# Query weights written in overlapping groups of four columns, and 22 agents copied with shifts from rows four partitions apart

## The chip, the cores and the metric

The kernel runs on one core of one Trainium2 chip. A core has five engines with a queue of instructions each: TensorE (PE in the profile; its weight loads, PEld, run beside its matmuls), VectorE (DVE), ScalarE (ACT), GpSimd (POOL) and SyncE (SP, which here issues all but one of the DMA transfers), and 16 DMA engines that carry the transfers. The metric is the time of one execution in microseconds. Three runs of the kernel before gave 426.61, 426.80 and 429.79 us; their median is 426.8 us.

## The reference

Agent attention, then a gated convolution, for 4 batches of 12800 rows of 128 channels, 49 agents and 5 taps. What is computed, in float32:

```
def sm(a, b):
    s = scale * (a @ b.transpose(0, 2, 1))
    s = s - s.max(-1, keepdims=True)
    e = np.exp(s)
    return e / (e.sum(-1, keepdims=True) + 1e-09)
a2k = sm(agents, k)
agent_v = a2k @ v
q2a = sm(q, agents)
x = q2a @ agent_v
...
for k in range(K):
    gate_pre += conv_w[k][None, None, :] * xp[:, k:k + S, :]
gate = 1.0 / (1.0 + np.exp(-gate_pre))
val = x @ w_val
return gate * val @ w_out
```

`xp` is `x` with four rows of zeros ahead of it: tap k reads a row k - 4 back.

## The kernel before, in words

**Units and chunks.** A batch is cut into 10 units of 1280 rows for the attention and 25 chunks of 512 rows for the convolution. Two units make a segment of 2560 rows, which is five chunks.

**The two halves.** For each batch, keys and values are first reduced to 49 agent vectors (`key_scores`, `key_max`, `agent_values`). `fold_weights` then multiplies these vectors with the taps and with the value weights, so that gate and value come from the query weights (49 numbers a row) directly, without x itself. The keys and values of batch b + 1 run among the chunks of batch b.

**Two-part numbers.** The folded weights and the query weights w are each written as a float16 high part and a float16 rest, and three of the four products are summed: high with high, low with high, high with rest. With 128 rows of one tile, x1, a matmul covers the low part of w (49 rows), its high part (49 rows), and a second copy of the high part for as many agents as still fit (30 rows). The other 19 agents' high parts, for the product with the weights' rest, lie in a second tile, x2, each five times, shifted by 0 to 4 columns: 95 rows, so that one matmul does all five taps. A gate chunk is thus five matmuls with x1 (line 922) and one with x2 (line 926); a value chunk is one with each (949, 953). The output projection is three more (992 to 994), on hh and hl, the two parts of h.

**One unit of queries** (`queries`): scores on TensorE, a transpose and a maximum on VectorE, subtraction on GpSimd, exp on ScalarE, sums and division on VectorE into qw. Then pt, the tile of 128 columns, is filled: the high part by ScalarE (line 779), the second copy by GpSimd (784), the low part by GpSimd as w less the high part (794).

**Transposes and shifts.** The first four units' pt is transposed on TensorE, the others' by a DMA transpose from pt into x1 (line 835). When both units of a segment have landed, two DMAs on SP's queue copy the 19 agents with their shifts from x1 into x2 (`shifts`, line 884): 15 rows three partitions apart, then 4 neighbouring rows, each row read five times. This is called the shift pair here; the profile shows it as x<-x. (For the first four units there is a pair for every unit, of half the width.) A halo copy of four columns goes on GpSimd from one segment's x1 to the next one's (819); it waits for the transpose of the segment's second unit.

**What sets the order.** TensorE's order is written out by hand in a string. The instructions of all other engines and of SP's queue are put in order by a planner (`Plan.order`), which simulates the engines with a cost in microseconds that each step names; other costs give another order. Each queue then runs strictly in its order. SP's queue holds the loads of keys, queries and values (ld, a ring of 11), the transposes, the shift pairs and the writes of the output (ob).

Of the kernel before, what the change touches and what calls it, by code (L numbers as in the profile page):

```python
# [9 lines left out]
F32 = mybir.dt.float32  # L10
# [3 lines left out]
ALU = mybir.AluOpType  # L14
# [3 lines left out]
P = 128  # L18
G = 4
BLK = 32  # L20
AP_ = 64

UNIT = 1280
NBLK = 10
# [8 lines left out]
THREES = 15  # L33
NDUP = 2 * THREES
X2R = 19
X2CUTS = ((0, THREES, 3, 0.5), (THREES, X2R, 1, 0.3))
# [140 lines left out]
def tile_agent_attention_gated_conv(  # L177
# [39 lines left out]
    qw = ring(NPT, [P, NBLK, A], F32, "qw")  # L217
# [43 lines left out]
    tiny = const.tile([P, NBLK], F32, name="tiny")  # L261
    nc.scalar.dma_start(out=ag_sb, in_=agT)
# [5 lines left out]
    nc.vector.memset(tiny, 1e-9 / QS)  # L268
    nc.vector.memset(x1s[0][:, 0:PAD], 0.0)
    for t in wst_sb:  # L270
        nc.gpsimd.memset(t[:, TAPS + 1 :, :], 0.0)
# [232 lines left out]
    avT = const.tile([P, A], F32, name="avT")  # L504
    mx = const.tile([P, 2], F32, name="mx")
    gw = const.tile([P, TAPS, A], F32, name="gw")
    gs = const.tile([P, TAPS, A], F32, name="gs")
# [5 lines left out]
    def fold_weights(b):  # L513
# [19 lines left out]
        def normalise():  # L533
            dve.tensor_scalar_add(den, pt[:, 0:A], 1e-9)
            dve.reciprocal(out=den, in_=den)
            dve.tensor_tensor(out=avT, in0=pt[:, AP_ : AP_ + A], in1=den, op=ALU.mult)
# [5 lines left out]
                out=gw, in0=avT.unsqueeze(1).to_broadcast([P, TAPS, A]),  # L542
                in1=conv_sb.unsqueeze(2).to_broadcast([P, TAPS, A]), op=ALU.mult,
# [4 lines left out]
        def gate_scale():  # L548
# [16 lines left out]
                out=pv[:, 0:A], lhsT=wval_sb, rhs=avT, start=True, stop=True  # L565
# [4 lines left out]
        x2g = wst[:, TAPS + 1, 0 : TAPS * X2R].rearrange("p (r k) -> p k r", k=TAPS)  # L570
        x2v = wst[:, TAPS + 2, 0 : TAPS * X2R].rearrange("p (r k) -> p k r", k=TAPS)
        ghi = wst[:, 0:TAPS, 0:A]
        vhi = wst[:, TAPS, 0:A]

        def threes(x):

            if len(x.shape) == 2:
                return x[:, 0 : 3 * THREES].rearrange("p (i r) -> p i r", r=3)
            return x[:, :, 0 : 3 * THREES].rearrange("p k (i r) -> p k i r", r=3)

        def rest(out, full, s, hi):
            dve.scalar_tensor_tensor(
                out=out, in0=full, scalar=rs[:, s : s + 1], in1=hi,
                op0=ALU.mult, op1=ALU.subtract,
            )

        def val_weights():
# [9 lines left out]
            dve.tensor_scalar_mul(vhi, pv[:, 0:A], rs[:, 1:2])  # L597
            pv3, hi3 = threes(pv[:, 0:A]), threes(vhi)
            rest(
                wst[:, TAPS, 2 * A :].rearrange("p (i r) -> p i r", r=2),  # L600
                pv3[:, :, 0:2], 1, hi3[:, :, 0:2],
            )
            rest(x2v[:, HALO, 0:THREES], pv3[:, :, 2], 1, hi3[:, :, 2])
            rest(x2v[:, HALO, THREES:], pv[:, 3 * THREES : A], 1, vhi[:, 3 * THREES :])

        def gate_weights():
            dve.tensor_scalar_mul(ghi, gw, rs[:, 0:1])
# [6 lines left out]
        def gate_rest_pool():  # L614
            def less(out, full, hi):
                nc.gpsimd.tensor_tensor(out=out, in0=full, in1=hi, op=ALU.subtract)

            gs3, hi3 = threes(gs), threes(ghi)
            twos = wst[:, 0:TAPS, 2 * A :].rearrange("p k (i r) -> p k i r", r=2)
            for r in range(2):  # L620
                less(twos[:, :, :, r], gs3[:, :, :, r], hi3[:, :, :, r])
            less(x2g[:, :, 0:THREES], gs3[:, :, :, 2], hi3[:, :, :, 2])
            less(x2g[:, :, THREES:], gs[:, :, 3 * THREES :], ghi[:, :, 3 * THREES :])

        def gate_rest():
            gw3, hi3 = threes(gw), threes(ghi)
            twos = wst[:, 0:TAPS, 2 * A :].rearrange("p k (i r) -> p k i r", r=2)
            for r in range(2):
                rest(twos[:, :, :, r], gw3[:, :, :, r], 0, hi3[:, :, :, r])
            rest(x2g[:, :, 0:THREES], gw3[:, :, :, 2], 0, hi3[:, :, :, 2])  # L630
            rest(x2g[:, :, THREES:], gw[:, :, 3 * THREES :], 0, ghi[:, :, 3 * THREES :])
# [3 lines left out]
        if b == 0:  # L635
            add("pool", 0.4, gate_scaled, ["gw", "rsg"], ["gs"])
            add("act", 0.4, lambda: nc.scalar.copy(out=ghi, in_=gs), ["gs"], [(*w_, "g")])
            add("pool", 1.0, gate_rest_pool, ["gs", (*w_, "g")], [(*w_, "r")])
        else:
# [4 lines left out]
            lambda: nc.scalar.copy(out=wst[:, 0:TAPS, A : 2 * A], in_=ghi),  # L644
# [3 lines left out]
            "act", 0.22, lambda: nc.scalar.copy(out=wst[:, TAPS, A : 2 * A], in_=vhi),  # L648
# [84 lines left out]
    def queries(b, u):  # L733
# [4 lines left out]
        sT, d, e, w, r, sm = sts[x], qw[g % NPT], qw[g % NPT], qw[g % NPT], qr[x], qsm[x]  # L738
# [23 lines left out]
        def sums():  # L762
# [14 lines left out]
        p_ = ("pt", g % NPT)  # L777
        add(
            "act", 0.58, lambda: nc.scalar.copy(out=pt[:, :, A : 2 * A], in_=w),  # L779
# [3 lines left out]
            "pool", 0.44,  # L783
            lambda: nc.gpsimd.tensor_scalar(
                out=pt[:, :, 2 * A :].rearrange("p n (i r) -> p n i r", r=2),
                in0=w[:, :, 0 : 3 * THREES].rearrange("p n (i r) -> p n i r", r=3)[:, :, :, 0:2],
                scalar1=1.0, scalar2=0.0,
                op0=ALU.mult, op1=ALU.add,
# [3 lines left out]
        add(  # L792
            "pool", 1.09,
# [393 lines left out]
```

## Time and profile before

| | |
|---|---|
| median of 3 runs | 426.8 us (426.61 to 429.79) |
| span of the profiled execution | 423.6 us |
| what the fastest run has beyond that span | 3.0 us |
| TensorE busy | 403.9 us, 95% |
| ScalarE busy | 301.5 us, 71% |
| VectorE busy | 293.3 us, 69% |
| GpSimd busy | 228.2 us, 54% |
| DMA | 127.62 MB, 301 GB/s on average |
| shift pair of a segment | 375 KB and 100 KB |

For the profiled execution there is no other time than its span, from its first to its last instruction; the runs' times have the start and the end around it too. Busy shares are means over stages: up to about 60 us the kernel waits for the first loads and the first fold, from then on TensorE has work nearly without a break. A matmul's end is modelled, and 512 columns are listed at about 380 ns though the next one starts about 216 ns later, so a busy TensorE is read from its holes, not from the sum of its durations. An idle time in brackets stands before the instruction, with what ended it.

### The profile page before, as it was taken

To read this page: it belongs to the slowest core of one execution; us is meant where nothing else is said; L and a number is where in the kernel's file an instruction comes from. 1 tells how busy PE (TensorE), PEld (TensorE's weight loads), DVE (VectorE), ACT (ScalarE), POOL (GpSimd) and SP (SyncE) were. 2 spreads that over 40 slices of the span, in tenths; PEclk is the share of its full clock that TensorE was granted. 3 is DMA by queue.
4 is the path that set the end of the run, shared out by engine and by line. 5 is a ranking of instruction groups with operands and counts; after the bars stand their busy time and mean duration, and the time that the engine had idled before them with its cause. 6 is when DMAs were issued, how large, how long until landed. Compare 5 with 4: busy or idle time off the path is not lost.

```text
span 423.6 us, 10042 instructions
## 1 busy us (share of the span) xinstructions
PE 403.9 (95%) x3907; PEld 197.0 (47%) x3907; DVE 293.3 (69%) x562; ACT 301.5 (71%) x521; POOL 228.2 (54%) x263
## 2 busy tenths in 40 slices
PE   4979999999999999999999899999999989999995
PEld 1358434346555443446555343335555534344443
DVE  3757899867875978667795575767765678676231
ACT  1564568779966777678876486778876567788776
POOL 1002557654657565554566355574366277877553
PEclk9969999999999999999999899999999999999998
DMA  8999999999999999999999999999999977755733
GB/s 320 420 417 411 370 367 353 301 295 310 412 293 283 346 317 362 304 278 356 351 379 324 271 299 370 314 332 302 296 393 322 239 196 161 199 163 176 205 121 124
DMA packets 75129, 127.62 MB, mean 301 GB/s; under 512 B 50466, under 2 KB 50850, under 8 KB 75084
## 3 DMA queue, kind: packets, MB, share of 16 engines
q1 hardware_dynamic: 74940, 126.87, 96.9%
q8 instruction: 30, 0.49, 0.5%
q10 hardware_dynamic: 144, 0.13, 0.2%
q14 instruction: 15, 0.12, 0.1%
HBM read 79.25 MB, written 26.21 MB: 249 GB/s over the span
## 4 chain that ended last, share of the span: by engine, by line
PE 78%; DMA 9%; DVE 8%; ACT 1%; POOL 1%; issue 1%; SPq 0%; POOLq 0%; DVEq 0%; ACTq 0%
PE gate L922 23%; PE sc L376 17%; PE av L480 10%; PE val L949 5%; PE out L992 5%; PE val L953 5%; PE gate L926 5%; PE out L993 4%; DMA ld<-kT 4%; PE out L994 4%; DMA x<-pt 3%; DMA x<-x 2%; DVE h L962 1%; DVE qw L772 1%; DVE qsm L763 1%
## 5 line engine op out<-in xcount | busy, mean ns | idle before, releaser
L973 POOL TENSOR_TENSOR hl<-h,hh 128x512 f16<-128x512 f32 (+1 forms) x101 | 116.9, 1158 | 96.1 <-ACT hh L968 96.0
L922 PE MATMUL gate<-x,stat 128*128 128x512 f16 (+1 forms) x500 | 125.2, 380 | 0.2 <-ACT th L935 0.2
L962 DVE SCALAR_TENSOR_TENSOR h<-th,val 128x512 f32<-128x512 f32 x100 | 67.8, 678 | 66.8 <-PE out L993 26.2
L376 PE MATMUL sc<-ld,ag_sb 128*32 128x320 f32 x1280 | 101.5, 447 | 7.6 <-DMA ld<-kT 7.0
L935 ACT ACTIVATE th<-gate,unscale 128x512 f32<-128x512 f32 x100 | 68.3, 683 | 33.3 <-PE gate L926 31.7
L1006 ACT ACTIVATE ob<-out,oscale 128x512 f32<-128x512 f32 x98 | 67.3, 687 | 21.3 <-PE out L994 20.1
L922 PEld LDWEIGHTS <-stat 128*128 128x128 f16 x505 | 46.3, 97 | 63.7 <-issue 14.8
L968 ACT CAST hh<-h 128x512 f16<-128x512 f32 (+1 forms) x101 | 61.5, 609 | 17.2 <-DVE h L962 16.4
L750 POOL TENSOR_TENSOR qw<-sT,qmx 128x490 f32<-128x490 f32 x40 | 41.4, 1035 | 47.6 <-DVE qmx L745 47.5
L376 PEld LDWEIGHTS sc<-ld,ag_sb 128*32 128x32 f32 x1280 | 36.7, 111 | 59.4 <-issue 25.7
L480 PE MATMUL av<-ld,eT 128*32 128x129 f32 (+1 forms) x1400 | 50.7, 279 | 1.0 <-DVE eT L386 1.0
L480 PEld LDWEIGHTS av<-ld,eT 128*32 128x32 f32 (+1 forms) x1400 | 47.1, 117 | 7.5 <-issue 2.5
L794 POOL TENSOR_TENSOR pt<-qw,pt 128x490 f16<-128x490 f32 x40 | 44.8, 1120 | 3.1 <-ACT pt L779 2.9
L471 ACT ACTIVATE e<-ks,kbias 128x320 f32<-128x320 f32 x80 | 39.3, 554 | 5.4 <-DVE eT L386 3.3
L386 DVE STREAM_TRANSPOSE sT<-sc 128x640 f32<-128x640 f32 x40 | 33.6, 839 | 13.4 <-PE sc L376 12.7
L402 ACT COPY ks<-sc 128x640 f32<-128x640 f32 x40 | 27.7, 691 | 21.2 <-PE sc L376 19.1
L386 DVE STREAM_TRANSPOSE eT<-e 128x640 f32<-128x640 f32 x40 | 33.5, 842 | 9.8 <-ACT e L471 5.2
L926 PE MATMUL gate<-x,stat 95*128 95x512 f16 x100 | 38.3, 383 | 1.5 <-DMA x<-x 1.5
L949 PE MATMUL val<-x,stat 128*128 128x512 f16 x100 | 38.2, 382 | 0.8 <-DVE h L962 0.6
L953 PE MATMUL val<-x,stat 95*128 95x512 f16 x100 | 38.1, 381 | 0.0
L994 PE MATMUL out<-hl,wo 128*128 128x512 f16 x98 | 37.0, 378 | 1.1 <-POOL hl L973 1.1
L992 PE MATMUL out<-hh,wo 128*128 128x512 f16 x98 | 37.3, 381 | 0.1
(130 smaller groups left out, 389.4 us busy)
## 6 DMA issues: line engine op xcount, KB each, us to landing
ld<-kT SPq DMA_DIRECT2D x40, 640.0 KB
ld<-qT SPq DMA_DIRECT2D x40, 640.0 KB
ld<-vP SPq DMA_DIRECT2D x39, 645.0 KB
outT<-ob SPq DMA_DIRECT2D x48, 512.0 KB
x<-x SPq DMA_DIRECT2D x18, 375.0 KB
x<-x SPq DMA_DIRECT2D x18, 100.0 KB
outT<-ob SPq DMA_DIRECT2D x3, 256.0 KB
x<-x SPq DMA_DIRECT2D x4, 187.5 KB
```

The source lines that it names most:

```text
L376: nc.tensor.matmul(out=out[g * BLK : (g + 1) * BLK, j, 0:GT], lhsT=ag_sb[:, b, j * BLK : (j + 1) * BLK], rhs=src[:, g * GT : (g + 1) * GT] ...
L386: nc.vector.transpose(out=out.rearrange("p n (j i) -> p j n i", j=2), in_=in_.rearrange("p j (n i) -> p j n i", i=BLK),)
L480: nc.tensor.matmul(out=av[o + j : o + j + cols, 0 : C + 1], lhsT=et[:, n, j : j + cols], rhs=vt[:, n, :], start=(u == 0 and n < 2), stop=( ...
L922: nc.tensor.matmul(out=pg, lhsT=stat[:, k, :], rhs=x1[:, c : c + w], start=(k == 0), stop=False,)
L926: nc.tensor.matmul(out=pg, lhsT=stat[0 : TAPS * X2R, TAPS + 1, :], rhs=x2[0 : TAPS * X2R, o2 : o2 + w], start=False, stop=True,)
L935: lambda: nc.scalar.activation(out=th, in_=pg, func=AF.Tanh, scale=unscale[:, 0:1]),
L949: nc.tensor.matmul(out=pv, lhsT=stat[:, TAPS, :], rhs=x1s[(b * NCH + n0 // CH) // 5 % NX][:, PAD + o2 : PAD + o2 + w], start=True, stop=False,
L953: nc.tensor.matmul(out=pv, lhsT=stat[0 : TAPS * X2R, TAPS + 2, :], rhs=x2[0 : TAPS * X2R, o2 : o2 + w], start=False, stop=True,)
L962: lambda: nc.vector.scalar_tensor_tensor(out=h, in0=th, scalar=1.0, in1=pv, op0=ALU.add, op1=ALU.mult),
L968: "act", 0.16 + 0.42 * scale, lambda: nc.scalar.copy(out=hh, in_=h),
L973: lambda: nc.gpsimd.tensor_tensor(out=hl, in0=h, in1=hh, op=ALU.subtract),
L1006: lambda: nc.scalar.activation(out=ob[:, o : o + w], in_=po, func=AF.Copy, scale=oscale),
```

## The change

**Columns of pt.** pt's 128 columns get another layout. The high part stands in 17 groups of four neighbouring columns, from column 32 on; group i holds w of agents 3i - 1, 3i, 3i + 1, 3i + 2. Neighbouring groups overlap by one agent, so 16 agents stand twice. ScalarE writes all 680 elements a partition in one instruction; qw gets a zero column ahead of w and two behind it for the ends of the groups (52 columns for 49). GpSimd writes 11 more second copies (agents 0, 3, ... 30) to columns 21 to 31, where 30 stood before. The low part goes to the 51 columns that are left, in two GpSimd instructions of 210 and 300 elements; the second overwrites two columns that the first reads.

**Shifts.** 27 agents now stand twice in x1, so 22 go to x2, 110 rows, from row 16 on: 16 rows four partitions apart, then 6 rows four partitions apart. x2's other rows are zeroed once, and its matmuls use all 128 rows.

**Weights.** The folded weights take the same places: 51 columns for 49, two ScalarE copies for each low part instead of one, four subtractions for the value's rest instead of three.

**Costs.** The planner gets 0.75 for 0.58 (ScalarE's copy), 0.3 for 0.44 and 1.3 for 1.09 (GpSimd), 0.5 and 0.2 a unit for 0.5 and 0.3 (the pair). The string of TensorE's order is the same.

```
-THREES = 15
-NDUP = 2 * THREES
-X2R = 19
-X2CUTS = ((0, THREES, 3, 0.5), (THREES, X2R, 1, 0.3))
+AW = 52
+HI = 32
+FOURS = 17
+LOWS = ((HI + 4 * FOURS - 2, 0, 10), (0, 10, FOURS - 10))
+TWICE = 11
+AGAIN = HI - TWICE
+X2R = 22
+X2O = 16
+X2CUTS = ((0, 16, HI + 2, 0.5), (16, X2R, HI + 1 + 4 * TWICE, 0.2))
+def fours(x):
+    return x[:, :, HI : HI + 4 * FOURS].rearrange("p n (i r) -> p n i r", r=4)
+def threes(x, first, n, width):
+    ap = [tuple(d) for d in x.ap]
+    return bass.AP(x.tensor, x.offset + first, ap[:2] + [(3, n), (1, width)])
...
     for t in wst_sb:
-        nc.gpsimd.memset(t[:, TAPS + 1 :, :], 0.0)
+        nc.gpsimd.memset(t, 0.0)
+    for t in x2s + qw:
+        nc.gpsimd.memset(t, 0.0)
...
+        def rests(full, hi, out, x2_, less):
+            n = X2R - 16
+            less(out[:, :, HI + 4 : HI + 4 * FOURS : 4], full[:, :, 2:A:3], hi[:, :, 0:16, 3])
+            less(out[:, :, AGAIN:HI], full[:, :, 0 : 3 * TWICE : 3], hi[:, :, 0:TWICE, 1])
+            less(x2_[:, :, 0:16], full[:, :, 1:A:3], hi[:, :, 0:16, 2])
+            less(x2_[:, :, 16:], full[:, :, 3 * TWICE : A : 3], hi[:, :, TWICE : TWICE + n, 1])
+        def lows(out, hi):
+            for to, i0, n in LOWS[::-1]:
+                nc.scalar.copy(
+                    out=out[:, :, to : to + 3 * n].rearrange("p k (i r) -> p k i r", r=3),
+                    in_=hi[:, :, i0 : i0 + n, 1:4],
+                )
...
-            "act", 0.58, lambda: nc.scalar.copy(out=pt[:, :, A : 2 * A], in_=w),
+        hi = fours(pt)
+            "act", 0.75, lambda: nc.scalar.copy(out=hi, in_=threes(wide, 0, FOURS, 4)),
...
-            "pool", 0.44,
+            "pool", 0.3,
             lambda: nc.gpsimd.tensor_scalar(
-                out=pt[:, :, 2 * A :].rearrange("p n (i r) -> p n i r", r=2),
-                in0=w[:, :, 0 : 3 * THREES].rearrange("p n (i r) -> p n i r", r=3)[:, :, :, 0:2],
-                scalar1=1.0, scalar2=0.0,
-                op0=ALU.mult, op1=ALU.add,
+                out=pt[:, :, AGAIN:HI], in0=w[:, :, 0 : 3 * TWICE : 3],
+                scalar1=1.0, scalar2=0.0, op0=ALU.mult, op1=ALU.add,
             ),
...
-            "pool", 1.09,
-            lambda: nc.gpsimd.tensor_tensor(
-                out=pt[:, :, 0:A], in0=w, in1=pt[:, :, A : 2 * A], op=ALU.subtract
-            ),
+        def lower():
+            for to, i0, n in LOWS[::-1]:
+                nc.gpsimd.tensor_tensor(
+                    out=pt[:, :, to : to + 3 * n].rearrange("p n (i r) -> p n i r", r=3),
+                    in0=threes(wide, 1 + 3 * i0, n, 3), in1=hi[:, :, i0 : i0 + n, 1:4], op=ALU.subtract,
+                )
+        add("pool", 1.3, lower, [("qw", g % NPT), (*p_, 0)], [(*p_, 1)])
...
-        for r0, r1, every, us in X2CUTS:
-            first = A + (2 if every == 3 else 3 * THREES)
-            rows = x1[first : first + 1 + (r1 - r0 - 1) * every : every, c : c + 1]
+        for r0, r1, first, us in X2CUTS:
+            rows = x1[first : first + 1 + (r1 - r0 - 1) * 4 : 4, c : c + 1]
...
-                    out=x2[r0 * TAPS : r1 * TAPS, o : o + n * UNIT],
+                    out=x2[X2O + r0 * TAPS : X2O + r1 * TAPS, o : o + n * UNIT],
...
-                out=pg, lhsT=stat[0 : TAPS * X2R, TAPS + 1, :],
-                rhs=x2[0 : TAPS * X2R, o2 : o2 + w], start=False, stop=True,
+                out=pg, lhsT=stat[:, TAPS + 1, :], rhs=x2[:, o2 : o2 + w],
+                start=False, stop=True,
```

**Where the order moves.** Three places. The first is SP's queue ahead of the shift pair of chunk 20 of the second batch; ld from qT and kT are loads of queries and keys, DMA_TRANSPOSE goes from pt into x1, the two rows into x_105 are the pair, outT is the output. Before:

```order
L369 DMA ld_70<-kT 128x1280
L835 DMA_TRANSPOSE x_1_102<-pt_99 128x10x128
L369 DMA ld_71<-kT 128x1280
L835 DMA_TRANSPOSE x_1_102<-pt_100 128x10x128
L1021 DMA outT<-ob_123 128x1024
L369 DMA ld_61<-kT 128x1280
L369 DMA ld_62<-qT 128x1280
L884 DMA x_105<-x_1_102 75x1x2560
L884 DMA x_105<-x_1_102 20x1x2560
```

After:

```order
L859 DMA_TRANSPOSE x_1_102<-pt_99 128x10x128
L1044 DMA outT<-ob_122 128x1024
L391 DMA ld_70<-kT 128x1280
L859 DMA_TRANSPOSE x_1_102<-pt_100 128x10x128
L391 DMA ld_71<-kT 128x1280
L391 DMA ld_61<-kT 128x1280
L1044 DMA outT<-ob_123 128x1024
L907 DMA x_105<-x_1_102 80x1x2560
L907 DMA x_105<-x_1_102 30x1x2560
L391 DMA ld_62<-qT 128x1280
```

The query load ld_62 moved from ahead of the pair to behind it, and the first transpose moved ahead of an output write. The second place is the same queue ahead of the pair of chunk 20 of the first batch. Before:

```order
L835 DMA_TRANSPOSE x_0_101<-pt_97 128x10x128
L835 DMA_TRANSPOSE x_0_101<-pt_98 128x10x128
L369 DMA ld_63<-qT 128x1280
L1021 DMA outT<-ob_122 128x1024
L369 DMA ld_64<-kT 128x1280
L884 DMA x_106<-x_0_101 75x1x2560
```

After:

```order
L859 DMA_TRANSPOSE x_0_101<-pt_97 128x10x128
L391 DMA ld_63<-qT 128x1280
L859 DMA_TRANSPOSE x_0_101<-pt_98 128x10x128
L1044 DMA outT<-ob_122 128x1024
L391 DMA ld_64<-kT 128x1280
L391 DMA ld_65<-qT 128x1280
L907 DMA x_106<-x_0_101 80x1x2560
```

One query load moved ahead of the second transpose, another ahead of the pair. The third place is GpSimd's queue in the third batch, around the halo copy into x_0_101 (hl is the rest of h, pt_97 a unit's columns). Before:

```order
L973 TENSOR_TENSOR hl_119<-h_113,hh_116 128x512
L784 TENSOR_SCALAR pt_97<-qw_89 128x10x30
L794 TENSOR_TENSOR pt_97<-qw_89,pt_97 128x10x49
L819 COPY x_0_101<-x_3_104 128x4
L973 TENSOR_TENSOR hl_117<-h_111,hh_114 128x512
L973 TENSOR_TENSOR hl_118<-h_112,hh_115 128x512
```

After:

```order
L996 TENSOR_TENSOR hl_119<-h_113,hh_116 128x512
L996 TENSOR_TENSOR hl_117<-h_111,hh_114 128x512
L807 TENSOR_SCALAR pt_97<-qw_89 128x10x11
L843 COPY x_0_101<-x_3_104 128x4
L816 TENSOR_TENSOR pt_97<-qw_89,pt_97 128x10x21
L816 TENSOR_TENSOR pt_97<-qw_89,pt_97 128x10x30
L996 TENSOR_TENSOR hl_118<-h_112,hh_115 128x512
```

One hl moved from behind the halo copy to ahead of it, and the unit's low parts moved behind it.

85 lines of the change are left out of this document (34 added, 51 removed).

## The prediction

> **What bounds the kernel now.** I read the page's busy line first, then the windows by stage, then the groups by form for the waits inside TensorE's holes, then the chain and the queue rows at those holes.
>
> ```profile
> span 423.6 us, 10042 instructions
> PE 403.9 (95%) x3907; PEld 197.0 (47%) x3907; DVE 293.3 (69%) x562; ACT 301.5 (71%) x521; POOL 228.2 (54%) x263
> ...
> 60.00:130.00 70.00, 69.93 (x747) 33.70 (x746) 55.79 (x94) 55.71 (x98) 43.73 (x47) 1.00 1.07 333
> 130.00:230.00 100.00, 100.00 (x1040) 48.13 (x1042) 75.04 (x141) 75.91 (x133) 57.93 (x65) 1.00 1.09 326
> 230.00:240.00 10.00, 8.50 (x107) 4.72 (x100) 5.10 (x14) 3.67 (x7) 4.97 (x7) 0.85 1.14 290
> 240.00:250.00 10.00, 10.00 (x84) 4.63 (x83) 7.23 (x21) 7.23 (x14) 5.70 (x8) 0.98 1.11 270
> 250.00:330.00 80.00, 80.00 (x840) 37.83 (x842) 56.60 (x102) 61.85 (x108) 44.26 (x49) 1.00 1.08 334
> 330.00:350.00 20.00, 18.31 (x166) 9.12 (x155) 13.68 (x38) 11.57 (x22) 10.46 (x14) 1.00 0.95 209
> 350.00:410.00 60.00, 59.84 (x328) 25.48 (x326) 35.15 (x60) 47.77 (x80) 41.82 (x44) 1.00 0.64 171
> ```
>
> A row gives the stretch, its length, the busy time of TensorE, weight loads, VectorE, ScalarE and GpSimd, then TensorE's granted clock, the DMA share and GB/s. TensorE is full from 60 to 410 us but for two holes: 1.50 us in 230 to 240 and 1.69 us in 330 to 350. At the first the clock falls too: (1 - 0.85) x 10 + (1 - 0.98) x 10 = 1.7 us of matmul time. The DMA engines are full up to 330 us as well. So a change that touches ScalarE, GpSimd and the transfers can give, after the first 60 us, what these holes hold, and can take more.
>
> ```profile
> L926 PE MATMUL gate<-x,stat 95*128 95x512 f16 x99 | 38.0, 384 | 1.5 <-DMA x<-x 1.5
> L949 PE MATMUL val<-x,stat 128*128 128x512 f16 x99 | 37.9, 383 | 0.8 <-DVE h L962 0.6 <-DVE wo L728 0.2
> L994 PE MATMUL out<-hl,wo 128*128 128x512 f16 x98 | 37.0, 378 | 1.1 <-POOL hl L973 1.1
> L819 POOL COPY x<-x 128x4 f16<-128x4 f16 x16 | 3.0, 187 | 16.9 <-DMA x<-pt 16.4 <-issue 0.5
> ...
> 220.73 7.50 DMA x<-pt
> 228.22 0.02 SPq L884
> 228.25 0.03 issue
> 228.28 7.34 DMA x<-x
> ...
> 236.89 2.24 PE gate L922 x5
> ...
> 243.56 1.19 PE gate L922 x5
> ...
> 338.78 0.19 POOL L819 COPY x<-x 128x4 f16<-128x4 f16 x1 [5.99 <-DMA x<-pt]
> 338.93 2.27 POOL L973 TENSOR_TENSOR hl<-h,hh 128x512 f16<-128x512 f32 x2
> ```
>
> The holes have two owners. The first is the shift pair (line 884): the gate's sixth matmul waits 1.5 us for the copy with shifts, issued at 228.28 and landed 7.34 us later, behind a transpose that itself took 7.50. Right after, five gate matmuls take 2.24 us where they otherwise take 1.19. The second is GpSimd's queue: the halo copy stands 5.99 us until a DMA transpose lands, and hl, which stands behind it, keeps the output matmul waiting 1.1 us; the 0.6 us on h follows from the same knot. Sum of what could go: 1.5 + 1.7 + 1.1 + 0.6 = 4.9 us.
>
> **The shift pair.** Its price alone is seen where the queue is nearly quiet; the window 382.7 to 385.9 us has one pair, in slices of 0.08 us, and loads at full flow stand beside it.
>
> ```profile
> DMA  9999769995993962396604371043310013401000
> ...
> DMA packets 129, 0.49 MB, mean 152 GB/s; under 512 B 34, under 2 KB 34, under 8 KB 129
> ...
> 10.00:20.00 10.00, 9.32 (x120) 3.72 (x111) 7.54 (x15) 4.88 (x8) 0.00 (x0) 1.00 1.02 419
> ```
>
> 475 KB (375 and 100) take 3.2 us at 152 GB/s; loads run at 419. The digits say why: full for twelve slices, then a long tail with few engines at work. The pair now carries 80 + 30 rows of 5 KB, 550 KB. Bounds: 550 KB at 419 GB/s = 1.3 us, at 152 GB/s = 3.7 us. I take 2.0: the first burst is 1.0 us long and most engines are done with their rows in it; if the tail is made of rows that get in each other's way, two transfers without it are two such bursts. That is 1.2 us less per pair. [...]
>
> **The order of the transfers.** SP issues in order. At the first hole, chunk 20 of the second batch, the orders shown with the change have one query load (ld from qT) moved from ahead of the pair to behind it: 640 KB at 419 GB/s = 1.6 us. With 1.2 from the pair and 0.4 lost on pt (below) it lands 2.4 us earlier where 1.5 are needed: the wait goes, 0.9 us to spare. What is late next there is the transpose, and the gate's first five matmuls don't wait for it now. At chunk 20 of the first batch the loads move the other way: two more stand ahead of the pair, 3.2 us at full flow.
>
> ```profile
> 127.74 1.67 SPq L884 DMA_DIRECT2D x<-x  x2
> ...
> 135.69 0.38 PE L926 MATMUL gate<-x,stat 95*128 95x512 f16 x1
> ```
>
> Issued at 127.74 and as long under way as the other (7.34), it lands at 135.1; it is used at 135.69. Slack 0.6, and 3.2 + 0.4 - 1.2 = 2.4 later: a new wait of 1.8, unless the queue has gained by then. Six pairs stand before it (four of half width); 4 x 0.6 + 2 x 1.2 = 4.8 us of queue are saved, and the DMA share is at or over 1 all that time, so I take the wait as covered and keep it as a rival.
>
> **The halo on GpSimd.** In the order of GpSimd at the second hole (third place shown), the hl that the output matmul waited for now stands ahead of the halo copy: 1.1 + 0.6 go. The next hl behind the copy is wanted a chunk later, about 2.4 us; if the transpose lands no earlier, up to that is hidden.
>
> **What the steps cost.**
>
> ```profile
> L968 ACT CAST hh<-h 128x512 f16<-128x512 f32 x99 | 60.7, 614 | 17.1 <-DVE h L962 16.4
> L968 ACT CAST hh<-h 128x256 f16<-128x256 f32 x2 | 0.8, 400 | 0.1
> L779 ACT CAST pt<-qw 128x490 f16<-128x490 f32 x40 | 23.9, 600 | 10.7 <-DVE qw L772 10.7
> L973 POOL TENSOR_TENSOR hl<-h,hh 128x512 f16<-128x512 f32 x99 | 115.5, 1168 | 94.8 <-ACT hh L968 94.7
> L973 POOL TENSOR_TENSOR hl<-h,hh 128x256 f16<-128x256 f32 x2 | 1.3, 671 | 1.3 <-ACT hh L968 1.3
> L794 POOL TENSOR_TENSOR pt<-qw,pt 128x490 f16<-128x490 f32 x40 | 44.8, 1120 | 3.1 <-ACT pt L779 2.9
> L784 POOL TENSOR_SCALAR pt<-qw 128x300 f16<-128x300 f32 x40 | 18.2, 457 | 20.6 <-DVE qw L772 20.6
> L648 ACT COPY wst<-wst 128x49 f16<-128x49 f16 x4 | 0.9, 229 | 0.0
> L582 DVE SCALAR_TENSOR_TENSOR wst<-av,rs,wst 128x15 f16<-128x15 f32 x3 | 0.8, 253 | 0.0
> L271 POOL MEMSET wst<- 128x256 f16 x2 | 0.6, 312 | 0.0
> L922 PE MATMUL gate<-x,stat 128*128 128x512 f16 x495 | 124.5, 381 | 0.2 <-ACT th L935 0.2
> ...
> POOL qw L750 <- DVE qmx L745: 47.5, 15, 32.9
> ```
>
> ScalarE's cast goes from 490 to 680 elements: (614 - 400) / 256 = 0.84 ns an element, 186 fixed, so 755 ns, 155 more, 6.2 us over 40 units. GpSimd's low parts become 210 and 300 elements: 1.94 ns an element, 174 fixed, 582 + 756 = 1338 against 1120, 218 more. The second copy shrinks from 300 to 110 elements: between the 457 and none, about 0.23 us less, so GpSimd's sum stays. The second low part waits for the first to end, since it overwrites two columns that the first reads; behind it stand the next hl and halo copies, and only the transposes wait for it. pt is ready 155 + 218 = 0.37, with that hand-over about 0.4 us later. All this lies beside a full TensorE; ScalarE has 29% to spare. Bounds for ScalarE's share on the path: 0 and 6.2; I take 0.3. For the first four units TensorE itself transposes pt, so one such 0.4 counts. The weight chain has one VectorE step more (0.25) and two ScalarE copies more (2 x 0.23) per batch, on the path only in the first, and there partly beside GpSimd's four subtractions, which stay at 245 elements: 0.2, between 0 and 0.7. The zeroing at the start grows from 512 to 11,808 elements, at 1.2 ns at most 14 us on GpSimd; GpSimd's idle 32.9 us ahead of its first query step hide it, so 0; without that cover, 14. The shift matmuls keep 512 columns: 384 ns with 95 rows and 381 for the full ones (L922), 3 x 200 ns, 0 to -0.6; I take 0. The wider qw holds the same 10 x 49 working elements, and 51 for 49 columns in the weight chain is 4% of short steps: nothing. Costs: 0.3 + 0.4 + 0.2 = 0.9.
>
> Against the profiled execution: 423.6 - 4.9 + 0.9 = 419.6 us of span. The runs' median, 426.8, lies 3.2 above that span: 422.8.
>
> **The rivals.** *Base*, 422.8; its own range is 420.6 (no costs, -0.6 on the matmuls, 0.7 of small waits gone with the queue) to 424.5 (the weight chain at its bound, 0.5, and a fifth of ScalarE's, 1.2).
> *The transpose sets the first hole* (its 7.50 us stand ahead of the pair, and pt is later): the wait and the clock stay, only the halo goes: 426.8 - 1.7 + 0.9 = 426.0.
> *The clock falls anyway.* In the rows it falls just behind the 1.5 us wait, and not behind the 1.1 us one. If the light matmuls there and not the wait bring it down, 1.7 stays: 424.5. [...]
> *A new wait at the first batch's chunk 20*: 1.8, and by the first hole's pattern 1.7 of clock: 426.3.
> *Slower: the pair keeps its rate.* At 152 GB/s it takes 3.7, 0.5 more. At the first batch's chunk 20 it is 3.2 + 0.4 + 0.5 - 0.6 = 3.5 late, with the clock 5.2; at the first hole it comes 1.6 - 0.5 - 0.4 = 0.7 earlier, so 0.8 and the clock stay. 426.8 + 5.2 - 0.7 - 1.7 + 0.9 = 430.5. It decides from a pair that takes 3.2 us or more alone; the tail's shape speaks against it.
> *Slower: ScalarE on the path*, all 6.2: 422.8 - 0.3 + 6.2 = 428.7; for it, th and ob each wait in a chain with TensorE; against it, its 71%.
>
> **How the numbers follow.** Base 0.60, of which 0.36 under 422.5; transpose 0.10; clock 0.06; new wait 0.10; rate 0.07; ScalarE 0.07. About 1% (4.3 us) is what a measurement of this kernel can tell from no change. Faster 0.36; within 0.24 + 0.26 = 0.50; slower 0.14. The range 420.6 to 427.7 takes in all cases but the last two and leaves about 0.06 below.
>
> **What would show it.** Right: the pair in the quiet part in about 2 us and near full flow; no wait of the gate for x<-x; one clock dip less after 230 us; no wait of the output matmul on hl near 338. Wrong: a tail still in the pair, a wait at the first batch's chunk 20, the cast far from 755 ns, or holes of TensorE on th or ob.

## The result, and the profile after

The changed kernel takes 430.43 us in the median (20 runs, 425.38 to 433.95), the kernel before, timed beside it, 427.12 (20 runs). The ratio is 1.0063, with a 95% interval from 1.0036 to 1.0089: 0.6% slower, 2.7 us of 427. (The medians are over all runs, the ratios leave disturbed runs out, so the two need not agree to the last digit; below, the ratio is used.) The prediction was 422.8, from 420.6 to 427.7.

The page of the changed kernel begins so; its profiled execution took 430.64 us.

```profile
span 427.8 us, 10101 instructions
PE 403.9 (94%) x3907; PEld 196.0 (46%) x3907; DVE 297.6 (70%) x567; ACT 307.6 (72%) x529; POOL 243.5 (57%) x310
```

TensorE's busy time is that of before to the tenth, 403.9. The span is 4.2 us longer, so the time went into TensorE's waits. The windows show where (columns as in the prediction: the stretch, its length, busy time of the five engines, granted clock, DMA share, GB/s).

```profile
60.00:130.00 70.00, 67.22 (x727) 32.31 (x726) 53.88 (x92) 52.90 (x92) 41.12 (x54) 0.98 1.08 328
130.00:230.00 100.00, 99.17 (x1020) 47.66 (x1019) 72.89 (x139) 76.64 (x133) 60.00 (x76) 1.00 1.08 333
230.00:240.00 10.00, 10.00 (x128) 5.54 (x126) 5.86 (x11) 6.93 (x13) 6.22 (x9) 1.00 1.27 280
250.00:330.00 80.00, 78.13 (x807) 36.98 (x800) 53.67 (x96) 59.37 (x102) 43.12 (x54) 0.98 1.08 333
330.00:350.00 20.00, 19.96 (x185) 9.93 (x184) 13.44 (x39) 13.83 (x26) 12.21 (x17) 1.00 0.92 227
...
97.00:100.00 3.00, 3.00 (x33) 1.37 (x36) 0.32 (x1) 2.59 (x6) 1.16 (x1) 0.52 1.22 237
305.00:308.00 3.00, 3.00 (x48) 2.23 (x44) 1.54 (x2) 2.95 (x7) 2.17 (x2) 0.50 1.05 271
```

The two holes of before are full now: 10.00 of 10 from 230 to 240, 19.96 of 20 from 330 to 350. Two others have opened, 2.78 us in 60 to 130 and 1.87 in 250 to 330, and about 3 us at half the clock stand behind each (last two rows). A smaller one of 0.83 us lies in 130 to 230. The groups by form say who waits there.

```profile
L949 PE MATMUL gate<-x,stat 128*128 128x512 f16 x99 | 37.7, 381 | 3.8 <-DMA x<-x 3.8
L1017 PE MATMUL out<-hl,wo 128*128 128x512 f16 x98 | 37.1, 379 | 1.9 <-POOL hl L996 1.9
L816 POOL TENSOR_TENSOR pt<-qw,pt 128x300 f16<-128x300 f32 x40 | 30.3, 758 | 3.1
L802 ACT CAST pt<-qw 128x680 f16<-128x680 f32 x40 | 30.2, 755 | 11.1 <-DVE qw L794 10.8
L816 POOL TENSOR_TENSOR pt<-qw,pt 128x210 f16<-128x210 f32 x40 | 24.8, 619 | 4.6 <-ACT pt L802 4.6
L843 POOL COPY x<-x 128x4 f16<-128x4 f16 x16 | 3.0, 188 | 17.6 <-DMA x<-pt 17.6
```

They are the same two kinds of wait as before, at other places and larger: the gate's sixth matmul waits 3.8 us for shift pairs (1.5 before), the output matmul 1.9 us for hl (1.1). Of the 3.8 us, 1.08 stand at 50.4 us, before these windows, and 2.70 at chunk 10; here is the chain there.

```profile
81.74 6.48 DMA x<-pt
...
88.24 0.61 SPq L907
...
88.90 7.76 DMA x<-x
...
96.71 0.61 PE gate L949
97.32 2.29 PE sc L398 x16
```

The pair of chunk 10 is issued at 88.24 and lands at 96.7; before it was issued at 86.20 and landed at 93.67, 0.31 us ahead of its use. That slack was the smallest of any pair that nobody waited for, and the prediction did not reckon with it. The second wait is in GpSimd's timeline (start, busy time, instruction, in brackets the idle time ahead and who ended it).

```profile
294.61 1.43 POOL L816 TENSOR_TENSOR pt<-qw,pt 128x210 f16<-128x210 f32 x2
302.67 0.19 POOL L843 COPY x<-x 128x4 f16<-128x4 f16 x1 [6.63 <-DMA x<-pt]
302.82 1.15 POOL L996 TENSOR_TENSOR hl<-h,hh 128x512 f16<-128x512 f32 x1
```

It is the halo knot of before (5.99 us at 338.78), now 36 us earlier at another halo copy: GpSimd stands 6.63 us until a DMA transpose lands, and the hl of chunk 59 stands behind it.

The lone pair did get faster. In the quiet part, 387.2 to 389.7 us in slices of 0.06 us:

```profile
DMA  9939959559989369639530290206605505320000
...
DMA packets 145, 0.56 MB, mean 225 GB/s; under 512 B 35, under 2 KB 35, under 8 KB 145
```

550 KB take 2.4 us, where 475 KB took 3.2; a thinner tail is left, from about 388.4 us on.

### The profile page after: what moved, and what is told of

The parts are those of the page before. It is cut to its first block, busy times and chain, and to the rows that moved or that the text cites. A ratio compares the mean times of both kernels' runs of the same rounds, so it can differ in the third digit from the quotient of the medians.

```text
span 427.8 us, 10101 instructions
## 1 busy us (share of the span) xinstructions
PE 403.9 (94%) x3907; PEld 196.0 (46%) x3907; DVE 297.6 (70%) x567; ACT 307.6 (72%) x529; POOL 243.5 (57%) x310
## 3 DMA queue, kind: packets, MB, share of 16 engines
q1 hardware_dynamic: 75336, 128.41, 95.5%
## 4 chain that ended last, share of the span: by engine, by line
PE 65%; DMA 13%; DVE 10%; issue 4%; ACT 3%; POOL 2%; SPq 1%; POOLq 0%; DVEq 0%
PE gate L945 19%; PE sc L398 14%; PE av L502 8%; DMA ld<-vP 6%; PE val L972 4%; PE out L1015 4%; PE val L976 4%; PE gate L949 4%; PE out L1016 4%; PE out L1017 4%; DMA x<-x 4%; DVE h L985 2%; DMA ld<-kT 2%; DVE qsm L785 2%; DMA x<-pt 2%
## 5 line engine op out<-in xcount | busy, mean ns | idle before, releaser
L398 PE MATMUL sc<-ld,ag_sb 128*32 128x320 f32 x1280 | 104.0, 455 | 8.1 <-DMA ld<-kT 7.2
L816 POOL TENSOR_TENSOR pt<-qw,pt 128x210 f16<-128x210 f32 x80 | 55.0, 688 | 7.8 <-ACT pt L802 4.6
L502 PEld LDWEIGHTS av<-ld,eT 128*32 128x32 f32 (+1 forms) x1400 | 46.1, 116 | 9.1 <-issue 3.4
L949 PE MATMUL gate<-x,stat 128*128 128x512 f16 x100 | 38.0, 380 | 3.8 <-DMA x<-x 3.8
L972 PE MATMUL val<-x,stat 128*128 128x512 f16 x100 | 37.9, 379 | 0.9 <-DVE h L985 0.7
L802 ACT CAST pt<-qw 128x680 f16<-128x680 f32 x40 | 30.2, 755 | 11.1 <-DVE qw L794 10.8
L976 PE MATMUL val<-x,stat 128*128 128x512 f16 x100 | 37.8, 378 | 0.0
```

What stands on the lines that cost most here:

```text
L398: nc.tensor.matmul(out=out[g * BLK : (g + 1) * BLK, j, 0:GT], lhsT=ag_sb[:, b, j * BLK : (j + 1) * BLK], rhs=src[:, g * GT : (g + 1) * GT] ...
L502: nc.tensor.matmul(out=av[o + j : o + j + cols, 0 : C + 1], lhsT=et[:, n, j : j + cols], rhs=vt[:, n, :], start=(u == 0 and n < 2), stop=( ...
L816: nc.gpsimd.tensor_tensor(out=pt[:, :, to : to + 3 * n].rearrange("p n (i r) -> p n i r", r=3), in0=threes(wide, 1 + 3 * i0, n, 3), in1=hi ...
L949: nc.tensor.matmul(out=pg, lhsT=stat[:, TAPS + 1, :], rhs=x2[:, o2 : o2 + w], start=False, stop=True,)
L972: nc.tensor.matmul(out=pv, lhsT=stat[:, TAPS, :], rhs=x1s[(b * NCH + n0 // CH) // 5 % NX][:, PAD + o2 : PAD + o2 + w], start=True, stop=False,
```

## The experiments

Each kernel was timed beside the kernel before. This table has the ratios to it, with 95% intervals; a per cent is 4.3 us.

| kernel | ratio | interval |
|---|---|---|
| changed | 1.0063 | 1.0036 to 1.0089 |
| e_zero: before, with the zeroing | 0.9983 | 0.9958 to 1.0009 |
| e_light: changed, most zeroing off GpSimd | 1.0116 | 1.0079 to 1.0153 |
| b_late: before, cast and low parts longer | 1.0008 | 0.9983 to 1.0032 |
| e_halo: changed, one halo copy later | 1.0047 | 1.0017 to 1.0077 |
| e_order: changed, old order | 1.0059 | 1.0024 to 1.0093 |
| a_thin: changed, pairs of 95 rows | 0.9955 | 0.9927 to 0.9983 |
| o_thin: changed, old order, 95 rows | 0.9927 | 0.9894 to 0.9959 |
| b_wide: before, 110 rows, 7 of 22 partitions neighbours | 1.0450 | 1.0410 to 1.0490 |
| b_step4: before, rows 4 apart from 51 | 0.9977 | 0.9948 to 1.0006 |
| b_port: before, rows 4 apart from 34 | 0.9975 | 0.9946 to 1.0003 |
| b_port_wide: the same, 75 + 35 rows | 1.0118 | 1.0085 to 1.0152 |
| b_cut: before, rows 3 apart, 80 + 15 rows | 1.0027 | 1.0002 to 1.0052 |
| b_split: 4 apart from 34, 80 + 15 rows | 0.9903 | 0.9867 to 0.9938 |
| b_six: the same, 80 + 30 rows | 1.0065 | 1.0029 to 1.0102 |
| b_even: the same, 96 + 15 rows | 0.9987 | 0.9956 to 1.0018 |
| best: changed, old order, 95 rows without leaving products out | 0.9931 | 0.9906 to 0.9957 |
| best_new: the same in the new order | 1.0001 | 0.9972 to 1.0030 |

**The zeroing at the start.** e_zero adds the changed kernel's zeroing to the kernel before; e_light moves most of it from GpSimd to VectorE in the changed one, and clears less:

```diff
-    for t in wst_sb:
-        nc.gpsimd.memset(t, 0.0)
-    for t in x2s + qw:
-        nc.gpsimd.memset(t, 0.0)
+    for t in x2s:
+        nc.vector.memset(t.bitcast(F32), 0.0)
+    for t in wst_sb:
+        nc.gpsimd.memset(t.bitcast(F32), 0.0)
+    for t in qw:
+        nc.gpsimd.memset(t[:, :, 0:1], 0.0)
+        nc.gpsimd.memset(t[:, :, 1 + A :], 0.0)
```

> The kernel before with the zeroing of the changed one added on GpSimd, and nothing else of the change (the query weight buffers are 490 wide, not 520). Theory (the zeroing costs by itself): the weights' first step is blocked to about 11.4 us, the first exponentials come 0.7 us later, and since the pair at chunk 10 landed with 0.3 us to spare, a wait of some 0.4 us or more stands there; 0.7 to 2.5 us slower than before. Rival (hidden): the first step is blocked all the same, but the time stays within 0.5 us of before.

> The changed kernel with its zeroing kept off GpSimd: VectorE clears the shift buffers as 32-bit words while it waits for the first load, GpSimd clears the weight buffers as 32-bit words and only the three spare columns of each query weight buffer; nothing else and no order changes. Theory (the zeroing blocks VectorE from 4.4 to 11.4 us, the key maxima end 0.7 us later and the whole queue with them): the first two-operation step of the weights takes 0.5 us again, not 7.0, the first exponentials start near 24.2 us, not 24.9, and the wait of the gate for the shift pair at chunk 10 falls from 2.7 us to under 2; the time falls by 0.7 to 3 us against the changed kernel, to 427.5 to 429.7. Rival (the start is hidden behind the loads, as the prediction had it): the start of the first chunk stays and so does the wait at chunk 10; 430.4, within 0.5.

In the timeline of e_zero VectorE is blocked as expected:

```profile
3.54 6.58 POOL L273 MEMSET x<- 128x2560 f16 x3
4.56 7.69 DVE L298 TENSOR_SCALAR ob<-ob 128x261 int32<-128x261 int32 x2 [2.97 <-DMA ob<-moe]
10.06 1.85 POOL L273 MEMSET qw<- 128x490 f32 x4
```

Its time is 0.9983 of before (0.9958 to 1.0009), so the block costs nothing that can be measured; the theory of the two expectations falls. With most of the zeroing off GpSimd VectorE's first two steps take 0.43 us, yet the kernel is slower than the changed one (1.0116), not faster. Its first chunk starts at 48.4 us, within the 47.5 to 49.9 of all kernels here. Why it is slower stayed open; its profile only shows more waits, most of them after 300 us (2.50 us without work for TensorE from 330 to 350, where the changed kernel has 0.04).

**The longer steps.** b_late writes ScalarE's cast and GpSimd's low parts in two instructions each, which makes pt as late as in the changed kernel.

```diff
-            "act", 0.58, lambda: nc.scalar.copy(out=pt[:, :, A : 2 * A], in_=w),
+            "act", 0.58, lambda: [
+                nc.scalar.copy(out=pt[:, :, A + i : A + j], in_=w[:, :, i:j]) for i, j in ((0, 30), (30, A))
+            ],
...
```

> The kernel before with ScalarE's cast of the query weights and GpSimd's low parts each written in two instructions (30 and 19 columns), so that pt is complete about 0.37 us later for every unit and ScalarE has some 0.19 and GpSimd 0.18 us more work a unit; result, transfers and order as before. Theory (the prediction's term for the longer steps): within 1 us of before, 427. Rival (later weights make the transposes late, and those set the queue): 2 to 4 us slower, 429 to 431.

1.0008: 0.3 us, between -0.7 and 1.4. The prediction's term for these steps holds, and the prediction's rival with all of ScalarE's 6.2 us on the path falls.

**The halo copy.** e_halo moves one instruction in the order of the changed kernel.

```diff
+    order = plan.order()
+    order.remove(names["halo", 14])
+    order.insert(order.index(names["hl", 59]) + 1, names["halo", 14])
-    for i in plan.order():
+    for i in order:
```

> The changed kernel with one instruction moved in GpSimd's queue: the halo copy of segment 14, which stood ahead of the hl of chunk 59 and waits for a DMA transpose until 302.7 us, now stands behind it. Theory (the knot of the kernel before has moved to here): the output matmul no longer waits 1.9 us for hl near 302 us, the clock drop behind it goes too; 3.6 us less than the changed kernel, 426.9. If the clock drop comes from elsewhere: 1.9 less, 428.5. Rival (the next step behind the copy is late in its turn): 430, a wait of the same size within 5 us of it.

The wait near 302 us is gone, the time is 1.0047 against 1.0063, a difference that the intervals don't tell from none. What came instead stands 40 us later in GpSimd's timeline, and in the group of the gate's first matmuls:

```profile
335.03 0.35 POOL L807 TENSOR_SCALAR pt<-qw 128x110 f16<-128x110 f32 x1
339.63 0.19 POOL L845 COPY x<-x 128x4 f16<-128x4 f16 x1 [4.25 <-DMA x<-pt]
...
342.28 0.61 POOL L562 TENSOR_TENSOR gw<-avT,moe_sb 128x255 f32<-128x255 f32 x1
...
L948 PE MATMUL gate<-x,stat 128*128 128x512 f16 x495 | 124.5, 382 | 3.0 <-ACT th L961 2.9
```

A later halo copy stands 4.25 us for its transpose (0.71 in the changed kernel, where TensorE had stopped at 302). Behind it stands gw, behind gw VectorE's weights, behind those a copy on ScalarE, and behind that the th that a gate matmul waits for, 2.2 us. That is the rival's kind of wait, but 40 us on where the rival had 5; and the time, 2.0 us over before (0.7 to 3.3), doesn't tell its 430 from the 428.5 of the theory without the clock. What the trace shows is that a TensorE freed of one halo copy was held up by a later one: that transpose lands at 339.6, when the queue gets to it.

**The order and the rows.** e_order plans the changed kernel with the old costs of its steps, which gives every queue the order of before. a_thin and o_thin cut the pair to 95 rows, in the new and the old order; they leave out the low products of three columns.

```diff
         for r0, r1, first, us in X2CUTS:
+            r1 = min(r1, 19)
```

> The changed kernel planned with the old costs of its steps, so that every queue has the order of the kernel before while the instructions are those of the changed one. Theory (two causes: the wait at chunk 10 comes from later weights, later start and a queue no shorter; the wait of the output matmul on hl near 302 us from the order alone): the wait at chunk 10 stays at 2 to 3 us with its clock drop, the one near 302 us goes (1.9 and 1.7 less), and the waits of the kernel before at chunk 20 of the second batch and near 338 us come back (3.2 and 1.7 more): 430.4 to 432. Rival (the new order alone cost it): about as before, 427. Rival (the new instructions as such are the gain the prediction saw, and the order lost it): under 426.

> The changed kernel with the second transfer of each pair cut from 30 rows to 15, so that a pair carries 95 rows as before; the low products of three columns are left out of the result. Theory (bytes in the queue): the time falls by 2.5 to 4.5 us against the changed kernel, to about 427; the wait for the pair at chunk 10 falls from 2.7 us to 2 or less and the transposes of units 26 to 29 land 3 us earlier. Rival (order and later weights): 430, with the waits at chunk 10 and near 302 us as they were. If the step of four partitions helped under load as well, under 424.

> The changed kernel in the old order of its queues and with pairs of 95 rows (the low products of three columns left out): what is left of the change is the longer cast, the two low parts, the step of four partitions and the start. Theory (bytes in the queue are nearly all of the loss): as before, 426 to 427.5. Rival (the longer steps make pt and the transposes late by themselves): as with the old order and 110 rows, 429. If the step of four helps under load: under 425.

The old order with 110 rows takes 1.0059, so the new one costs 0.2 us there, which the intervals don't tell from nothing. Without the 15 rows a_thin takes 0.9955 and o_thin 0.9927: the rows cost 4.6 us in the new order (plus or minus 1.6) and 5.6 in the old (plus or minus 2.0), against 2.5 to 4.5 that were expected of a_thin. In a_thin, with the order of the changed kernel, its two waits are gone:

```profile
L950 PE MATMUL gate<-x,stat 128*128 128x512 f16 x99 | 37.5, 379 | 0.0
L1018 PE MATMUL out<-hl,wo 128*128 128x512 f16 x98 | 37.1, 379 | 0.0
```

These are the rows that had 3.8 and 1.9 us. One part of e_order's expectation fell: the wait at chunk 10 did not stay (the pair lands 1.5 us ahead of its use), while those of before came back, 2.6 us at chunk 20 of the second batch and 1.0 on hl. TensorE's busy time from 60 to 330 us, for before, the changed kernel, e_order and o_thin in turn:

```profile
60.00:330.00 270.00, 268.42 (x2806) 129.01 (x2808) 199.76 (x370) 204.37 (x356) 156.58 (x173) 0.99 1.08 327
60.00:330.00 270.00, 264.51 (x2753) 127.52 (x2752) 195.68 (x365) 203.45 (x351) 155.79 (x198) 0.99 1.08 330
60.00:330.00 270.00, 266.07 (x2786) 128.00 (x2775) 198.41 (x370) 206.44 (x358) 161.88 (x205) 1.00 1.08 328
60.00:330.00 270.00, 269.99 (x2867) 131.16 (x2865) 201.72 (x375) 209.75 (x363) 164.20 (x207) 1.00 1.08 331
```

In o_thin it is full. The rest of the change, then, with as many bytes as before, gains 3.1 us (1.8 to 4.5).

The traces also show where the order counts. In the five with the new order (the changed kernel, e_halo, e_light, a_thin, best_new) the pair of chunk 20 of the second batch lands 2.6 to 4.6 us ahead of its use; in those with the old order it lands 1.2 us ahead at the most, whatever it carries, and in most of them the gate waits. At chunk 20 of the first batch, where the new order has two more loads ahead of the pair, the gate waits 0.77, 0.98 and 0.84 us in e_halo, e_light and best_new. One trace of a kernel is one execution, though: e_zero has the order and the transfers of before, and in its trace the gate doesn't wait at the pair where it waited 1.50 us before.

**Which rows.** b_step4, b_port and b_wide take other rows of x1 in the kernel before, or more of them. b_port reads every fourth partition from 34 in the first transfer and every fourth from 77 in the second, as many rows and bytes as before; its low products are not the right ones. Its edit:

```diff
-            first = A + (2 if every == 3 else 3 * THREES)
-            rows = x1[first : first + 1 + (r1 - r0 - 1) * every : every, c : c + 1]
+            first = 34 if every == 3 else 77
+            rows = x1[first : first + 1 + (r1 - r0 - 1) * 4 : 4, c : c + 1]
```

> The kernel before with the rows of each pair taken four partitions apart instead of three and one apart: same rows in number, bytes and places written, but other rows, so the low products are not the right ones. [...] Rival (the prediction's: what a pair saves alone it saves in the queue): 22 pairs at up to 1 us less, the wait at chunk 20 of the second batch goes with its clock drop: 424 or less. Rival (the tail has nothing to do with the step): the quiet pair stays at 3.2 us, 427.

> [...] Theory (a pair costs the full queue the busy time of the engines that carry it, summed and divided by 16: 95 packets of 288 ns are 1.7 us now, 95 of 237 ns would be 1.4): the quiet pair takes 2.3 to 2.7 us, its packets 240 ns, and the time falls by up to 20 x 0.3 = 6 us, to 421 to 425. [...]

> The kernel before, with three partitions more in the second transfer of each shift pair (35 rows instead of 20, into rows of the shift buffer that no matmul reads), so that a pair carries 110 rows as in the changed kernel; order and all else as before. Theory (the queue of transfers is what the kernel runs after up to 340 us, and a pair costs it by its bytes): 1.54 MB more at the 334 GB/s of the stretch from 60 to 330 us are 4.6 us, some 3.5 of them by the transpose of unit 29, which landed at 323.1 and now lands near 326.6; the time rises by 2.5 to 4.5 us, to about 430.5. Rival (the changed kernel lost its time to the new order and later weights): within 1 us of before, 427.

The lone pair takes 3.0 to 3.1 us in b_step4, 2.4 in b_port and 6.5 in b_wide; its packets of 5,120 bytes take 316, 244 and 402 ns (about 290 before, about 240 in the changed kernel). So it is not the step of four that shortens it, but where the rows lie: those of b_step4 are four apart too, from 51, and those of b_port from 34, as in the changed kernel; b_wide reads seven neighbours. Why the place counts no run shows. Under load it is another matter. b_step4 and b_port both take 0.9975 or so, 1 us less than before with an interval that holds zero, so the gain of 2 to 6 us that was expected of b_port is not there. b_wide, with the slowest lone pair, takes 19 us more, where 2.5 to 4.5 were expected:

```profile
L928 PE MATMUL gate<-x,stat 95*128 95x512 f16 x99 | 38.2, 386 | 13.6 <-DMA x<-x 13.6
```

**Bytes or spread.** In the completion events of the traces a second transfer of 3, 4, 6 or 7 partitions counts 4, 5, 7 or 8 events, from which the author estimates that a transfer lies on as many of the 16 engines as it has partitions. Five kernels with the order of before vary what the two transfers carry. Their rows are four apart as in b_port, from 34 in the first transfer; those of b_cut, which writes the second and third column of each group twice and copies the first, are three apart, with three neighbours in the second transfer. In all but b_cut the low products are not the right ones. b_port_wide has 75 + 35 rows, b_split and b_cut 80 + 15, b_six 80 + 30, b_even 96 + 15. All but b_port_wide have this cut:

```diff
-X2CUTS = ((0, THREES, 3, 0.5), (THREES, X2R, 1, 0.3))
+X2CUTS = ((0, 16, 3, 0.5), (16, X2R, 1, 0.3))
```

> [...] Rival (bytes alone): 4.6 us over before, 431. [...]

> [...]

> [...] Theory (the cut into 80 and 15 has most of the gain): 423 to 424.5, 0.6 to 0.9% faster than before. [...]

> [...] The kernel with 3 partitions (15 rows) in the second transfer took 421.65 us. Theory (the 15 rows are what the changed kernel lost): 426 to 428, 5 to 6 us more. Rival (the cut into 80 rows makes room for them): under 424.

> [...] In the completion events of the traces the second transfer of 3, 4, 6 and 7 partitions counts 4, 5, 7 and 8 events and the first of 16 partitions 16, so a transfer seems spread over as many of the 16 engines as it has partitions. Theory (bytes): 16 rows more cost what 15 more cost in the second transfer, 426 to 428. Rival (rows in the second transfer cost because they load only some engines on top of their share of the first): spread over all 16 engines they cost 2 us or less, under 424.

With 35 rows instead of 20 in the second transfer the time rises by 1.4% (6.1 us, b_port to b_port_wide), with 30 instead of 15 by 1.6% (6.9 us, b_split to b_six), although the lone pair hardly changes: 2.44 to 2.55 us in the first case. With 16 rows more spread over all partitions of the first transfer it rises by 0.8% (3.6 us, plus or minus 2.0; b_split to b_even). So the rows cost in part by their bytes and, by 3.3 us plus or minus 2.1 in this pair, by coming from few partitions. That it is the engines that count there is not shown: the rows of three partitions more also come from three places in x1, and no run takes the two apart. The group rows of b_split and b_six show where it is paid:

```profile
L926 PE MATMUL gate<-x,stat 95*128 95x512 f16 x99 | 37.7, 381 | 0.2 <-DMA x<-x 0.2
```

```profile
L928 PE MATMUL gate<-x,stat 95*128 95x512 f16 x99 | 38.0, 383 | 4.9 <-DMA x<-x 4.9
...
L996 PE MATMUL out<-hl,wo 128*128 128x512 f16 x98 | 37.0, 378 | 2.3 <-POOL hl L975 2.3
```

These are the changed kernel's two kinds of wait (of the 4.9 us, 1.10 at the first chunk, 2.36 at chunk 10 and 1.46 at chunk 20 of the second batch), in a kernel with the old steps and the old order. b_split, at 421.65 us in the median, is 1.0% faster than before; it has the first rows of b_port and the cut into 80 and 15 rows. b_port, without the cut, gains 0.25%, with an interval that holds zero. b_cut, with the cut alone, gains nothing (1.0027, where 0.6 to 0.9% less was expected), but its lone pair takes 3.4 us and more, with other rows than b_split's; so whether the cut would do it alone isn't told.

**A version with 95 rows and the whole result.** The first layout left three columns empty; "best" writes duplicates over them, so that GpSimd's second copy has 14 columns and stands behind the low parts, and 19 agents go by the pair.

```diff
-TWICE = 11
-AGAIN = HI - TWICE
-X2R = 22
+TWICE = 14
+AGAIN = HI + 1 - TWICE
+X2R = 19
...
-                out=pt[:, :, AGAIN:HI], in0=w[:, :, 0 : 3 * TWICE : 3],
+                out=pt[:, :, AGAIN : HI + 1], in0=w[:, :, 0 : 3 * TWICE : 3],
...
```

> [...] Rival (pt later by 0.3 us a unit costs what the rows gain): 426 to 428.

> The complete version with 95 rows and 14 columns written twice, now in the order of the changed kernel's queues instead of the old one. Theory (the order is worth nothing by itself): as with the old order, 423.5 to 425. Rival (the new order costs by itself, as 424.16 and 424.14 us with the same products left out could hide in their intervals): 425.5 to 427.

In the old order it takes 423.87 us in the median, 0.7% less than before and 1.3% less than the changed kernel: it beats both. In the new order it takes 1.0001. The new order costs 3.0 us here, plus or minus 1.7, so the expectation that it is worth nothing by itself fell. It cost 0.2 with 110 rows and 1.2 between o_thin and a_thin, and neither of these is told from nothing.

## Why the prediction was wrong

The change taken apart in the old order of the queues: -3.1 us for all but the extra rows (before to o_thin), +5.6 for the rows (o_thin to e_order), +0.2 for the order (e_order to the changed kernel), 2.7 in all. That they add up is no check, since each is taken from the one before; what carries the argument is the size of the rows' part, which other kernels show again as 4.6, 6.1 and 6.9 us. The -3.1 is not far from the -4.0 that was forecast, but by luck: it is measured without the moves in the order that the forecast counted on, and with them (a_thin) it is -1.9. b_split, which has the cut and rows four apart from 34 and nothing else of the change, gains 4.1.

**The step that failed** is the price of the pair: "That is 1.2 us less per pair", and behind it "4.8 us of queue are saved". The lone pair was sized well, 2.0 against 2.4 us, though no run shows the two bursts without a tail that the 2.0 was made of: rows still arrive 2.4 us after the start. But its duration is the time to its last row, when no one else wants the engines. In the queue, whose DMA share is at 1.08 from 60 to 330 us, 75 KB more in each pair cost 5 to 7 us over the run where the prediction had 1.2 us less per pair. The rows that said so were quoted: the queue moves 327 GB/s on average from 60 to 330 us, and the 1.54 MB that it carries more (128.41 against 126.87) are 4.7 us at that rate. The bound of 152 GB/s was an upper end for a lone pair, not for what it takes from others. So the queue came later, not earlier, and a covered wait opened: chunk 10 (slack 0.31) in place of chunk 20 of the second batch. The bytes don't account for all of that one: ahead of it only four pairs of half width had gone, 150 KB more, 0.5 us, and it is issued 2.0 us later. With 95 rows in the same order (a_thin) it is issued at 85.63 and lands 1.2 us ahead of its use; why the rows cost more than their bytes there stays open.

**The holes.** That both go is what the profile shows, and others opened in their place. In e_order, with the changed kernel's pair and the old order, the gate waits 2.6 us for it at 235 us, and the traces in the new order all have slack there; so the first hole went with the order. That it was the load moved behind the pair fits, but no run moves that load alone. The shorter lone pair had no part in it, since e_order has it too. The halo step was right where it looked ("the hl that the output matmul waited for now stands ahead of the halo copy") and failed in looking at the place of the old hole only: two others of the 16 halo copies had moved among the hl too, one of them ahead of the hl of chunk 59.

**The costs.** The cast is at 755 ns as predicted, the low parts at 758 + 619 = 1377 against 1338. That they cost almost nothing holds (b_late, 0.3 with an upper end of 1.4, against 0.7 without the weight chain). The zeroing at 0 holds too, but not for its reason: GpSimd's idle time hid GpSimd's part, and nothing was said of VectorE, which stands 7 us behind it.

**The rivals.** "The pair keeps its rate", the slower one, has the time, 430.5, by luck and not by its mechanism: the lone pair took 2.4 us and the first batch's chunk 20 kept its slack of 1.2 (134.49 to 135.69 before, where the prediction reckoned with 0.6). "A new wait" at that chunk is not in the changed kernel's trace, but in three other traces of the new order, at 0.8 to 1.0 us. The clock stays at 1.00 from 230 to 240 us in the changed kernel, so its drop there went with the wait; more on it below. The three together had 0.23.

What stays open: why e_light is slower than the changed kernel, how much of the order's 0.2 to 3.0 us belongs to which move, how the rows read and the cut share the 1.0% of b_split, and whether rows from few partitions cost more by the engines that carry them or by the places they are read from.

## What to carry to other kernels

Price a transfer alone only if it runs alone; in a full queue price it by its bytes (here 4.7 us for 1.54 MB at 327 GB/s, where 4.6 to 6.9 were measured), expect more if few partitions carry them (here 3.3 us, plus or minus 2.1, b_six against b_even), and check that against the smallest slack among all the waits that don't show yet. When a knot of a queue (here the halo copy ahead of hl) is taken out by a new order, look for it in the whole order and not at its old place. Where TensorE and the transfers are both full, a gap closed at one place can come back at the next transfer (as in e_halo, where the wait near 302 us went and one of 2.2 us came 40 us later) unless the transfers themselves become less.

## What the runs showed of the hardware

**Neighbouring rows in a full queue.** Three partitions more in the second transfer (35 rows for 20) cost 6.1 us when the rows lie four apart (b_port to b_port_wide) and 19 when they are neighbours (before to b_wide), although the bytes are the same.

**The clock after a wait.** After the waits of 1.50 us (before), 1.87 and 2.70 (changed) and 2.23 (e_halo) the granted clock is at half for some 3 us: 0.75 and 0.50 from 236 to 238 and 238 to 240 us (before), 0.50 from 305 to 308 and 0.52 from 97 to 100 (changed), 0.50 from 346 to 349 (e_halo). After waits as long it is not: this is e_order, whose pair kept the gate waiting 2.59 us at 235.

```profile
235.00:238.00 3.00, 0.41 (x3) 0.01 (x1) 1.05 (x3) 0.55 (x2) 0.74 (x1) 1.00 1.20 131
238.00:241.00 3.00, 2.99 (x16) 1.66 (x17) 1.64 (x5) 1.53 (x3) 0.33 (x1) 1.00 1.21 329
```

So 1.50 us of waiting was enough here and 2.59 us was too little; what decides it no run shows.

**GpSimd's zeroing and VectorE.** While GpSimd clears buffers, from 3.5 to 12 us, two VectorE steps that take 0.50 us before take 7.0 in the changed kernel and 7.7 in e_zero. Nothing of it that could be measured reached the end (e_zero, 0.9983).
